# Four idle products of 128 columns in place of eight of 64, and one SwiGLU unit with two split chunks in place of ten

## The chip, the cores and the metric

The kernel runs on one core of a Trainium2 chip. Its engines work side by side, each through its own list of instructions in order, and wait for each other by semaphores: TensorE (matrix products; the profile calls its products PE and its weight loads PEld), VectorE (DVE), ScalarE (ACT), GpSimd (POOL) and SyncE (SP), which issues the transfers here. The metric is the device time of one execution in microseconds; of several runs the median is given.

## The reference

Two blocks read the same normalised input and are added to it: linear attention with a softmax feature map (A) and a SwiGLU block (B). S = 2048 tokens, D = 640, H = 32 heads of 20, F = 1536, all in bfloat16.

```
xn = layernorm(x)
q, k, v   = heads of xn @ wqkv
phi(u)    = [softmax(u @ w_phi), softmax(-(u @ w_phi))]      per head, 40 features
kv, z     = sum over tokens of phi(k) (x) v, and of phi(k)
o         = (phi(q) @ kv) / (phi(q) @ z + 1e-6)
out = x + (o @ wo) + (silu(xn @ w1) * (xn @ w3)) @ w2
```

## The kernel before

The tokens are 16 tiles of 128; a SwiGLU unit works on 512 tokens (a quarter) and 128 of the 1536 hidden columns, so there are 48 units. The input columns are 5 chunks of 128, over which each product accumulates in PSUM. The order of the work on every engine is written out by hand (`tc.manual_schedule`, line 156): what stands first in the text runs first on its engine.

The stages follow each other in this order.

- **Start and V.** The first tiles are loaded and transposed on TensorE (`by_pe`, line 294), their row statistics taken, and V is computed; the first three tiles use the raw input and are corrected later. While TensorE has nothing to do, it multiplies a tile of zeros into a bank that nobody reads: `warm(n, cols)`, line 219, issues n products with `cols` columns, 128 if not told otherwise. 40 of 64 columns stand ahead of the first tile (line 226) and 8 of 64 between the transposes of the first and second tile (line 766).
- **K stage** (line 908). For each of 16 tiles: the feature product, six exponentials on ScalarE, sum and reciprocal on VectorE, the scaling on GpSimd, and two tiles later the products that sum phi(k) and v. In between TensorE works off SwiGLU units.
- **Q stage** (line 936). The same feature product with the weights of q, for t = 0 to 15; the last two tiles of the K sum come at t = 0 and 1. For t = 0 to 6 two SwiGLU units follow each tile (lines 944 to 946). The first unit at t = 0 goes through `fill_halves(gate, up)`, line 710: it computes a unit like any other, but the last `gate` of the 5 chunks of the gate product, and the last `up` of those of the up product, are each done as two products of 256 columns in place of one of 512 (line 719). With 5 and 5 all chunks are split. All other units have products of 512 columns (line 459). After the products, ScalarE takes the tanh of the gate (line 470) and VectorE multiplies it together (lines 487 and 490).
- **Output.** Twelve tiles are computed in transposed pieces (`out_piece`, line 646), four tiles straight (`out_unit`, line 590). The very last tile is added and stored in three parts.
- **The branch** (line 999). A safeguard computes norms of the fused weights and, if they are too large, runs a second, general form of the attention. The flag is known long before the end, but the branch comes last: with these inputs every engine jumps over the general form to the last addition and store (`finish`, line 1025).

Each product is two instructions on TensorE, a weight load and the product itself. The split chunks use the same weights twice, and the weights are loaded for each half.

Of the kernel before, what the change touches and what calls it, by code (L numbers as in the profile page):

```python
# [8 lines left out]
P = 128  # L9
# [3 lines left out]
def kernel(  # L13
# [53 lines left out]
    def bank(name, dt=f32):  # L67
        n = 512 if dt == f32 else 1024
        return psum.tile([P, n], dt, name=name, tag="bank")
# [75 lines left out]
    def ld(dst, src):  # L145
        nc.sync.dma_start(out=dst, in_=src)
# [9 lines left out]
    with tc.manual_schedule():  # L156
# [62 lines left out]
        def warm(n, cols=P):  # L219
            for _ in range(n):  # L220
                nc.tensor.matmul(idle[:, 0:cols], nought[:], nought[:, 0:cols])
# [19 lines left out]
        def ln_stats(*ts):  # L241
            made = []
            for t in ts:
                xt = xin[:, (t // 4) % 3, t % 4, :]
                st = work.tile([P, 2, 6], f32, name="st")
                for i in range(2):
                    nc.vector.bn_stats(out=st[:, i, :], in_=xt[:, i * HD : (i + 1) * HD])  # L247
                made.append(st)
            for t, st in zip(ts, made):
                nc.vector.bn_aggr(out=mv[:, t, :], in_=st[:])  # L250
# [43 lines left out]
        def by_pe(dst, t, ps):  # L294
            xt = xin[:, (t // 4) % 3, t % 4, :]
            for c in range(KD):
                nc.tensor.transpose(
                    ps[:, c * P : (c + 1) * P], xt[:, c * P : (c + 1) * P], ident[:]
                )
            for c0, c1 in ((0, 2), (2, KD)):  # L300
                nc.scalar.copy(
                    out=dst[:, c0:c1, t * P : (t + 1) * P],
                    in_=ps[:, c0 * P : c1 * P].rearrange("p (c s) -> p c s", s=P),
                )
# [43 lines left out]
        def tile_of(t):  # L348
            return slice(t * P, (t + 1) * P)
# [61 lines left out]
        def phi_unit(t, w, name, exps=exps, cols=None):  # L411

            ps = by_token(cols or tile_of(t), w, name, CH)
            dst = phi[:, t % 4]
            exps(ps, dst)
            rows = dst.rearrange("p c g f -> p (c g) f")[:, :, 0:60].rearrange(
                "p a (i d) -> p a i d", d=Dh
            )
            sk = work.tile([P, 2 * NCH, 3], f32, name="sk")
            nc.vector.reduce_sum(out=sk[:], in_=rows, axis=AX.X)  # L420
            rk = work.tile([P, 2 * NCH, 3], f32, name="rk")
            nc.vector.reciprocal(out=rk[:], in_=sk[:])  # L422
            nc.gpsimd.tensor_mul(  # L423
                out=rows, in0=rows, in1=rk[:, :, :, None].to_broadcast([P, 2 * NCH, 3, Dh])
            )
# [28 lines left out]
        def glu_unit(sc, fi, banks=None):  # L454

            gp, up = banks or (bank("gp")[:], bank("up")[:])
            for ps, w in ((gp, w1), (up, w3)):
                for c in range(KD):
                    nc.tensor.matmul(  # L459
                        ps,  # L460
                        w[:, c, fi * P : (fi + 1) * P],
                        xnT[:, c, sc * 512 : (sc + 1) * 512],
                        start=(c == 0),
                        stop=(c == KD - 1),
                    )
            return glu_done(sc, fi, gp, up)

        def glu_done(sc, fi, gp, up):
            th = work.tile([P, 512], f32, name="th")
            nc.scalar.activation(out=th[:], in_=gp, func=AF.Tanh, scale=0.5)  # L470
            return lambda: glu_product(sc, fi, gp, up, th)
# [24 lines left out]
        def kv_unit(t, v1, acc, first, last):  # L496

            for c in range(NCH):
                b, i = divmod(c, 6)
                nc.tensor.matmul(  # L500
                    acc[:, b, VC * i : VC * i + 1 + Dh * HC[c]],
                    phi[:, t % 4, c].rearrange("p g f -> p (g f)"),
                    v1[:, c, 0 : 1 + Dh * HC[c]],
                    start=(first and i == 0),
                    stop=last,
                    skip_group_check=True,
                )
# [77 lines left out]
        def residual(rows):  # L585
            xr = work.tile([P, D], bf, name="xr")
            ld(xr[:], x2[rows, :])
            return xr
# [83 lines left out]
        def group_stored(g, i):  # L672
            rows = out2[(4 * g + 2 * i) * P : (4 * g + 2 * i + 2) * P, :]
            ld(
                rows.rearrange("(t p) d -> p t d", p=P),
                y[:, 2 * i : 2 * i + 2].rearrange("p t c s -> p t (c s)"),
            )
# [28 lines left out]
        def fill(n):  # L706
            for _ in range(n):
                glu_unit(*glu.pop(0))()

        def fill_halves(gate, up):  # L710

            sc, fi = glu.pop(0)
            gp, upp = bank("gp")[:], bank("up")[:]
            for ps, w, whole in ((gp, w1, KD - gate), (upp, w3, KD - up)):
                for c in range(KD):
                    n = 1 if c < whole else 2
                    for i in range(n):
                        a, b = i * 512 // n, (i + 1) * 512 // n
                        nc.tensor.matmul(
                            ps[:, a:b],  # L720
                            w[:, c, fi * P : (fi + 1) * P],
                            xnT[:, c, sc * 512 + a : sc * 512 + b],
                            start=(c == 0),
                            stop=(c == KD - 1),
                            skip_group_check=True,
                        )
            glu_done(sc, fi, gp, upp)()
# [35 lines left out]

        pst = [bank("pst", bf), bank("pst", bf)]
        by_pe(xrT, 0, pst[0])
        warm(8, P // 2)
        ln_stats(0)
        ln_root(0)
        by_pe(xrT, 1, pst[1])
# [166 lines left out]
        for t in range(NST + 4):  # L936
            if t < NST:
                phi_unit(t, wqphi, "pq")
            if t < 2:
                kv_unit(turns[t - 2], vaug[:, turns[t - 2]], acc, False, t == 1)  # L940
                if t == 1:
                    kv_done([acc[:, 0], acc[:, 1]])
                    ld(w2, B_w2.rearrange("(c p) d -> p c d", p=P))
            if t < 7:
                (fill_halves(5, 5) if t == 0 else fill(1))
                fill(1)
            for g, c in pieces.get(t, []):
                out_piece(g, c)
            outs = {16: (12,), 19: (13, 14, 15)}.get(t, ())
            for j in outs:  # L950
                last = tile_of(j) if j == NST - 1 else None
                res = out_unit(hT[:, j], tile_of(j % 4), xrs[j], last)
                if j == 13:
                    group_stored(2, 0)
                    group_stored(2, 1)
                if 13 <= j < 15:
                    xrs[j + 1] = residual(tile_of(j + 1))
                if last is None:
                    ld(out2[tile_of(j), :], res[:])
            if 2 <= t < NST + 2:  # L960
                r_unit(t - 2)
            if t < NST:
                phi_transposed(t)
            if 2 <= t < NST + 2:
                o_transposed(t - 2, (t - 2) // 4)
            if t in backs:
                group_back(*backs[t])
            if t in (12, 13):
                group_stored(0, t - 12)
            if t == 17:  # L970
                group_stored(1, 0)
            if 2 <= t < 6:
                x_back(t - 2)
            if 7 <= t < 11:
                x_back(t - 3)
            if 13 <= t < 17:
                x_back(t - 5)
            if t == 15:
                xrs[12] = residual(tile_of(12))
            if t == 17:  # L980
                xrs[13] = residual(tile_of(13))
            if t == 18:
                group_stored(1, 1)
                group_back(2, 0)
                group_back(2, 1)
            if t < 4:
                norm_unit(wqphi, 1, t)
            if t == 4:
                ld(listed[:], norms[:])
                ld(flat, listed[:].rearrange("p g -> (p g)").partition_broadcast(1))  # L990
            if t == 10:
                flag_unit()
            if t == 12:
                ok = nc.values_load(flag[0:1, 0:1], min_val=0, max_val=1)
# [59 lines left out]
```

## Time and profile before

| | us |
|---|---|
| median of 3 runs | 270.57 |
| lowest, highest | 268.92, 271.35 |
| the profiled execution | 268.92 |
| its span, first to last instruction | 267.2 |
| TensorE products, busy | 260.3 (97% of the span) |
| weight loads, busy | 153.9 (58%) |
| VectorE, ScalarE, GpSimd, busy | 193.1, 113.6, 90.6 |

The duration of a product includes a tail in which the next one is already running, so the time that a product takes in a row of products is the difference between two starts. A few records of products are missing from a trace: it has 1895 weight loads and 1869 products. The granted clock of TensorE is 1.000 in the mean of the span.

### The profile page before, as it was taken

To read this page: it belongs to the slowest core of one execution; us is meant where nothing else is said; L and a number is where in the kernel's file an instruction comes from. 1 tells how busy PE (TensorE), PEld (TensorE's weight loads), DVE (VectorE), ACT (ScalarE), POOL (GpSimd) and SP (SyncE) were. 2 spreads that over 40 slices of the span, in tenths; PEclk is the share of its full clock that TensorE was granted. 3 is DMA by queue.
4 is the path that set the end of the run, shared out by engine and by line. 5 is a ranking of instruction groups with operands and counts; after the bars stand their busy time and mean duration, and the time that the engine had idled before them with its cause. 6 is when DMAs were issued, how large, how long until landed. Compare 5 with 4: busy or idle time off the path is not lost.

```text
span 267.2 us, 5059 instructions
## 1 busy us (share of the span) xinstructions
PE 260.3 (97%) x1869; PEld 153.9 (58%) x1895; DVE 193.1 (72%) x356; ACT 113.6 (43%) x349; POOL 90.6 (34%) x83
## 2 busy tenths in 40 slices
PE   8999999999999999999999999999999999999993
PEld 7766465655556555555665555555555555544663
DVE  5899964397876877799879999998899685305121
ACT  5864354746668744466765554324222420000000
POOL 5022720064643544433553333346336433000000
PEclk9999999999999999999999999999999999999999
DMA  6958757984000002400009859456776999354861
GB/s 189 320 155 170 133 120 167 346 133 98 1 2 0 1 3 20 157 0 0 2 4 290 166 110 116 88 128 76 151 162 69 190 217 169 99 101 95 194 201 32
DMA packets 82828, 31.25 MB, mean 117 GB/s; under 512 B 71279, under 2 KB 81391, under 8 KB 82800
## 3 DMA queue, kind: packets, MB, share of 16 engines
q1 hardware_dynamic: 82800, 30.89, 52.1%
q8 instruction: 16, 0.26, 0.4%
q14 instruction: 12, 0.10, 0.1%
HBM read 11.17 MB, written 2.63 MB: 52 GB/s over the span
## 4 chain that ended last, share of the span: by engine, by line
PE 96%; DMA 1%; issue 1%; SPq 0%; DVE 0%
PE up L459 18%; PE gp L459 18%; PE acc L652 15%; PE pq L357 8%; PE pk L357 8%; PE acc L598 7%; PE pv L357 7%; PE acc L657 6%; PE pr L535 2%; PE pkv L500 2%; DMA reg_w<-in_A_wqkv_dram 1%; PE pf L443 1%; PE pv L308 1%; PE up L476 1%; PE gp L476 1%
## 5 line engine op out<-in xcount | busy, mean ns | idle before, releaser
L423 POOL TENSOR_TENSOR phi<-phi,rk 128x1320 bf16<-128x1320 bf16 x32 | 77.2, 2412 | 108.8 <-DVE rk L422 87.2
L459 PEld LDWEIGHTS <-w 128*128 128x128 bf16 x450 | 42.6, 97 | 46.9
L420 DVE TENSOR_REDUCE sk<-phi 128x66 f32<-128x1320 bf16 x32 | 48.8, 1525 | 19.6 <-ACT phi L386 18.3
L459 PE MATMUL up<-xnT,w 128*128 128x512 bf16 x225 | 55.9, 379 | 0.1
L459 PE MATMUL gp<-xnT,w 128*128 128x512 bf16 x206 | 54.3, 378 | 0.9
L357 PEld LDWEIGHTS <-xnT 128*128 128x128 bf16 x450 | 42.8, 98 | 19.2
L386 ACT ACTIVATE phi<-pq 128x360 bf16<-128x360 f32 (+2 forms) x96 | 24.8, 366 | 42.1 <-issue 31.8
L652 PE MATMUL acc<-reg_h,reg_v 128*128 128x512 bf16 x180 | 41.3, 379 | 0.0
L470 ACT ACTIVATE th<-gp 128x512 f32<-128x512 f32 x48 | 29.2, 611 | 26.8 <-PE gp L459 23.7
L490 DVE SCALAR_TENSOR_TENSOR reg_h<-gs,up 128x512 bf16<-128x512 bf16 x48 | 33.0, 688 | 5.4 <-PE pv L357 0.5
L487 DVE SCALAR_TENSOR_TENSOR gs<-th,gp 128x512 bf16<-128x512 f32 x48 | 31.4, 654 | 4.7 <-ACT th L470 4.7
L386 ACT ACTIVATE phi<-pk 128x360 bf16<-128x360 f32 (+2 forms) x96 | 24.9, 370 | 19.4 <-PE pk L357 19.4
L652 PEld LDWEIGHTS <-reg_v 128*128 128x128 bf16 x180 | 17.4, 98 | 19.1
L357 PE MATMUL pk<-wkphi,xnT 128*128 128x360 bf16 (+1 forms) x160 | 24.3, 299 | 0.0
L357 PE MATMUL pq<-wqphi,xnT 128*128 128x360 bf16 (+1 forms) x160 | 24.3, 299 | 0.0
L422 DVE RECIPROCAL rk<-sk 128x66 f32<-128x66 f32 x32 | 18.1, 566 | 3.2
L357 PE MATMUL pv<-reg_w,xnT 128*128 128x360 bf16 (+1 forms) x130 | 18.6, 299 | 0.0
L607 DVE TENSOR_TENSOR res<-acc,xr 128x320 bf16<-128x320 f32 (+3 forms) x9 | 3.8, 451 | 15.9 <-PE acc L598 10.5
L247 DVE BATCH_NORM_STATS2 st<-reg_h 128x6 f32<-128x320 bf16 x32 | 13.4, 479 | 2.1 <-DMA reg_h<-in_A_x_dram 2.1
L372 ACT CAST reg_v<-pv 128x360 bf16<-128x360 f32 (+2 forms) x39 | 10.7, 349 | 9.7 <-PE pv L357 9.7
L660 DVE TENSOR_TENSOR w<-acc,v_raw 128x512 bf16<-128x512 f32 x10 | 6.6, 671 | 11.2 <-issue 6.2
L556 DVE TENSOR_TENSOR o__77<-pr,den 128x360 bf16<-128x360 f32 (+1 forms) x32 | 14.2, 486 | 0.6
(90 smaller groups left out, 211.7 us busy)
## 6 DMA issues: line engine op xcount, KB each, us to landing
w<-in_B_w_dram SPq DMA_DIRECT2D x2, 1280.0 KB, 6.6
reg_v<-in_B_w_dram SPq DMA_DIRECT2D x1, 1920.0 KB, 8.9
out_dram<-w SPq DMA_DIRECT2D x6, 320.0 KB, 2.7
reg_h<-in_A_x_dram SPq DMA_DIRECT2D x5, 320.0 KB, 5.1
w<-in_B_w_dram SPq DMA_DIRECT2D x4, 320.0 KB, 6.8
reg_h<-in_A_x_dram SPq DMA_DIRECT2D x6, 160.0 KB, 2.5
reg_w<-in_A_wqkv_dram SPq DMA_DIRECT2D x5, 160.0 KB, 3.5
reg_w<-in_A_wo_dram SPq DMA_DIRECT2D x1, 800.0 KB, 7.5
```

The lines of the kernel that those rows point to most:

```text
L357: nc.tensor.matmul(ps[i][:, 0 : b - a], xnT[:, c, cols], w[:, c, a:b], start=(c == 0), stop=(c == KD - 1), skip_group_check=True,)
L386: nc.scalar.activation(out=dst[:, c0 : c0 + n, g, 0:k], in_=p.rearrange("p (c f) -> p c f", c=n), func=AF.Exp, scale=1.0 - 2.0 * g,)
L420: nc.vector.reduce_sum(out=sk[:], in_=rows, axis=AX.X)
L422: nc.vector.reciprocal(out=rk[:], in_=sk[:])
L423: nc.gpsimd.tensor_mul(out=rows, in0=rows, in1=rk[:, :, :, None].to_broadcast([P, 2 * NCH, 3, Dh]))
L459: nc.tensor.matmul(ps, w[:, c, fi * P : (fi + 1) * P], xnT[:, c, sc * 512 : (sc + 1) * 512], start=(c == 0), stop=(c == KD - 1),)
L470: nc.scalar.activation(out=th[:], in_=gp, func=AF.Tanh, scale=0.5)
L487: nc.vector.scalar_tensor_tensor(out=gs[:], in0=th[:], scalar=1.0, in1=gp, op0=ALU.add, op1=ALU.mult)
L490: nc.vector.scalar_tensor_tensor(out=hT[:, 4 * sc : 4 * sc + 4, fi, :], in0=gs[:].rearrange("p (t s) -> p t s", t=4), scalar=0.5, in1=up.r ...
L598: nc.tensor.matmul(ps[:, 0 : b - a], rows[j][0], rows[j][1][:, a:b], start=(j == 0), stop=(j == len(rows) - 1),)
L652: nc.tensor.matmul(acc4, w2[:, k, cols], hT[:, 4 * g : 4 * g + 4, k, :], start=(k == 0), stop=False,)
L657: nc.tensor.matmul(acc[:], wo[:, k, cols], oTs[g][:, k, :], start=False, stop=(k == KD - 1),)
```

## The change

Two calls change. Between the transposes of the first two tiles, four idle products of 128 columns are issued in place of eight of 64, the same 512 columns. In the first SwiGLU unit of the Q stage only the last chunk of the gate product and the last of the up product are split; the other four of each are whole. TensorE thus issues four idle products and eight SwiGLU products fewer, each with its weight load, and computes the same values. No other engine's instructions change.

```
         pst = [bank("pst", bf), bank("pst", bf)]
         by_pe(xrT, 0, pst[0])
-        warm(8, P // 2)
+        warm(4)
         ln_stats(0)
...
             if t < 7:
-                (fill_halves(5, 5) if t == 0 else fill(1))
+                (fill_halves(1, 1) if t == 0 else fill(1))
                 fill(1)
```

More of the change, by code (lines that the diff above doesn't have):

```diff
@@ L765 @@
         by_pe(xrT, 0, pst[0])
-        warm(8, P // 2)
+        warm(4)
         ln_stats(0)
@@ L944 @@
             if t < 7:
-                (fill_halves(5, 5) if t == 0 else fill(1))
+                (fill_halves(1, 1) if t == 0 else fill(1))
                 fill(1)
```

## The prediction

> **What bounds the kernel now.** I read the page's shares, its clock row and its chain first, then who waits for whom on TensorE, then the stretches between the first wait and the last product.
>
> ```profile
> PE 260.3 (97%) x1869; PEld 153.9 (58%) x1895; DVE 193.1 (72%) x356; ACT 113.6 (43%) x349; POOL 90.6 (34%) x83
> ...
> PEclk9999999999999999999999999999999999999999
> ...
> PE 96%; DMA 1%; issue 1%; SPq 0%; DVE 0%
> ```
>
> TensorE is busy for 97% of the span and carries 96% of the chain that ended last; no other engine is above 72%. So the time is the sum of TensorE's products, unless something makes TensorE stand. The view of waits, for TensorE alone, has two rows:
>
> ```profile
> PE idle L225 <- PEq L1038: 0.8, 1, 0.8
> PE v L308 <- DMA reg_w<-in_A_wqkv_dram: 0.3, 1, 0.3
> ```
>
> The first is the launch, the second the wait for a piece of the V weights near the start. The chain in order of time begins and ends like this (start, duration, what; the first two rows are neighbours, the last is the end):
>
> ```profile
> 2.18 3.20 DMA reg_w<-in_A_wqkv_dram
> 5.42 0.43 PE v L308 x2
> ...
> 262.86 0.26 DVE res L607
> ```
>
> Before 5.42 us the chain is the weight transfer, not the products. From then on it is TensorE to 262.83 us. The view of stretches (length, busy time and count of PE, PEld, DVE, ACT, POOL, granted clock, DMA share, GB/s) gives its two parts:
>
> ```profile
> 5.42:262.83 257.41, 256.02 (x1807) 149.95 (x1832) 190.55 (x347) 110.62 (x343) 87.39 (x65) 1.00 0.53 117
> 262.83:267.20 4.37, 0.00 (x0) 0.00 (x0) 0.26 (x1) 0.00 (x0) 0.00 (x0) 1.00 0.08 21
> ```
>
> In 257.41 us TensorE shows 1.39 us without a product, with 1832 weight loads and only 1807 products. Every product has its own load, so 25 products are missing from the records; with no wait recorded there, I read the 1.39 us as those and not as standing. The profiled execution took 268.92 us: 5.42 to the first product that waited, 257.41 of products, 4.37 for the last addition, the last store and the end, and 1.72 outside the span (268.92 - 267.20). It is the lowest of the three runs; the median is 270.57 and the highest 271.35, a spread of 2.43 us (0.9%) that this profile cannot explain, since it is of the lowest run.
>
> **Part one: the idle products of the start.** The view of instructions in order of time, TensorE alone (start, duration, engine, line, operation, what, count):
>
> ```profile
> 1.05 2.32 PE L221 MATMUL idle<-nought 128*128 128x64 bf16 x40
> 3.18 0.72 PE L297 MATMUL pst<-ident,reg_h 128*128 128x128 bf16 x5
> 3.69 0.63 PE L221 MATMUL idle<-nought 128*128 128x64 bf16 x8
> 4.14 0.66 PE L297 MATMUL pst<-ident,reg_h 128*128 128x128 bf16 x5
> 4.64 0.43 PE L308 MATMUL v<-reg_w 128*128 128x360 bf16 x2
> 5.42 0.43 PE L308 MATMUL v<-reg_w 128*128 128x360 bf16 x2 [0.35 <-DMA reg_w<-in_A_wqkv_dram]
> 5.69 0.43 PE L308 MATMUL pv<-reg_w 128*128 128x360 bf16 x2
> 5.96 0.44 PE L297 MATMUL pst<-ident,reg_h 128*128 128x128 bf16 x5
> 6.24 0.43 PE L308 MATMUL pv<-reg_w 128*128 128x360 bf16 x2
> ```
>
> Durations include a tail that overlaps the next product, so I take differences of starts. The eight products of 64 columns go from 3.69 to 4.14: 0.45 us. Four of 128 columns have no row before the change; five transposes of 128 columns do. On either side of the edit they take 0.51 us (3.18 to 3.69) and 0.50 (4.14 to 4.64), 0.10 each; a little later 0.28 (5.96 to 6.24), 0.056 each. TensorE thus works at about half its later rate until after 4.14 us, though the granted clock stands at 9 tenths or more in all 40 slices. Four products are between 4 x 0.056 = 0.22 and 4 x 0.102 = 0.41 us; I take 0.41, because the edit sits between two groups at the slow rate. The change is -0.04 us, within -0.23 and 0. It is worth nothing: the products at 4.64 run out of weights and TensorE then stands idle for 0.35 us until 5.42, a moment that the transfer sets. Anything saved is added to that idle time. If the transfer came earlier in another run, at most the 0.04 would show. The four weight loads that go with the four products lie under products as well.
>
> **Part two: the SwiGLU unit at the first Q tile.** Same view, TensorE, ScalarE and VectorE around the unit:
>
> ```profile
> 132.40 0.49 PE L500 MATMUL pkv<-reg_v,phi 128*128 128x61 bf16 x11
> ...
> 132.74 1.25 PE L719 MATMUL gp<-xnT,w 128*128 128x256 bf16 x10
> ...
> 133.83 1.25 PE L719 MATMUL up<-xnT,w 128*128 128x256 bf16 x10
> 134.03 0.60 ACT L470 ACTIVATE th<-gp 128x512 f32<-128x512 f32 x1
> 134.13 1.53 DVE L420 TENSOR_REDUCE sk<-phi 128x66 f32<-128x1320 bf16 x1 [0.33 <-ACT phi L386]
> ...
> 134.92 1.24 PE L459 MATMUL gp<-xnT,w 128*128 128x512 bf16 x4
> ...
> 136.00 1.24 PE L459 MATMUL up<-xnT,w 128*128 128x512 bf16 x5
> ...
> 136.24 0.63 DVE L487 SCALAR_TENSOR_TENSOR gs<-th,gp 128x512 bf16<-128x512 f32 x1
> ```
>
> Ten products of 256 columns take 133.83 - 132.74 = 1.09 us for the gate and 134.92 - 133.83 = 1.09 for the up half. The next unit, by five products of 512, takes 136.00 - 134.92 = 1.08. Splitting costs 0.01 us per five products (rows have two decimals, so 0 to 0.02). After the change four of the five chunks are whole and one is split: 0.8 of that goes, twice: -0.016 us, bounds -0.03 and 0. This is on the path, as TensorE has no gap here. Eight loads fewer lie under the products. What hangs on the unit does not move it: the tanh starts when the gate ends and is done at 134.63, while VectorE, busy with its sum from 134.13, takes up the result only at 136.24. No transfer is issued or moved, no wait is added, and no other engine's program changes.
>
> **The sum.** 0 - 0.016 = -0.02 us, against the profiled execution 268.90. Set on the median instead, 270.57 - 0.02 = 270.55; I say **270.5**.
>
> **What the sum leaves out: the instructions themselves.** Four and eight products go, each with its load: 24 TensorE instructions. The page lists the transfers that bring instructions, and the view of the final branch's line lists what the sequencers do there (count, shortest, median and longest ns, first and last start us); the last row is SyncE's longest wait at the end:
>
> ```profile
> q8 instruction: 16, 0.26, 0.4%
> ```
>
> ```profile
> L999 ACTq COMPARE_BRANCH  x1: 50/50/50, 217.8 to 217.8; - x1
> L999 ACTq EVENT_SEMAPHORE  x1: 17/17/17, 219.2 to 219.2; - x1
> L999 POOLq COMPARE_BRANCH  x1: 45/45/45, 221.5 to 221.5; - x1
> L999 POOLq EVENT_SEMAPHORE  x1: 17/17/17, 223.9 to 223.9; - x1
> L999 PEldq COMPARE_BRANCH  x1: 1295/1295/1295, 261.9 to 261.9; - x1
> ...
> L999 PEldq EVENT_SEMAPHORE  x1: 51/51/51, 263.2 to 263.2; - x1
> ```
>
> ```profile
> SPq L1049 <- DMA out_dram<-res: 2.1, 1, 2.1
> ```
>
> Sixteen packets carry 0.26 MB, 16 KB each; 0.4% of 16 engines' 267.2 us is 17.1 us, 1.07 us a packet. If they are TensorE's, its 2 x 1895 products and loads make some 69 bytes an instruction, and 24 instructions move every later packet boundary by a tenth of a packet. TensorE shows no wait at any boundary now. At the end its jump takes 1.3 us (261.9 to 263.2); on ScalarE the next instruction comes 1.4 us after the jump (217.8 to 219.2), on GpSimd 2.4 (221.5 to 223.9). Were TensorE's jump as long as GpSimd's, it would end 1.1 us later, and SyncE waits 2.1 us for the last store anyway: nothing. So I cost the moved boundaries at zero, with -1.3 (a jump or a fetch that disappears where it was uncovered) and +2.4 as ends. The Trainium skill, "Runtime: NRT & Kernel Launch", section "Instruction fetch mechanics", says that an engine's instructions come in blocks of 16 KiB, that crossing a block is mostly hidden, and that a taken branch whose target isn't loaded forces a fetch. The packet size and the times at the branch agree with it. By its figure of 256 instructions a block, 24 would be 0.09 of one, and its rule alone would let the end change by a fetch.
>
> **The rivals.**
>
> **A block comes late (slower).** The boundary lands where TensorE runs dry, in the products or at the jump beyond its cover. For it: 24 instructions shift all boundaries after 132 us, and the branch does cost its engines 1.3 to 2.4 us. Against it: 16 packets, no wait. Price 1.07 to 2.4 us, the lower end being likelier: 270.55 + 1.07 = 271.6, up to 273.0. It decides from the point where a stand passes the 2.1 us of cover at the end, or is in the products at all. Chance 0.13.
>
> **The slow start lasts longer (slower).** If fewer instructions in the first microseconds count as less work, the half rate stays. It lasts about 3.8 us now (0.84 to 4.64). Again as long would add half of that, 1.9 us, less up to 0.35 of idle time: 1.55 to 1.9, that is 272.1 to 272.5. Against it: TensorE is as busy as before, 0.41 of 0.45 us. Chance 0.08. The Trainium skill, "TensorE: Matmul & The Clock Gate", Part 1, section "What's actually happening", says that a free-running window of about 3.4 us of busy time, and not a number of instructions, opens the clock. By that the edit would do nothing, and the phase would vary a run by up to 1.7 us (an estimate, half of that window). The step after 3.8 us agrees; that the phase varies, no run here shows.
>
> **Fewer stands than before (faster).** The two higher runs of before may hold a stand that the profiled one lacks, and moved boundaries may avoid it: 268.9 to 269.3, up to -1.6. For it: the spread of 2.43 us. Against it: nothing in the profile places it. Chance 0.12.
>
> **How the numbers follow.** No change has 0.67, with runs between 268.9 and 271.4 as they were. A measurement of this kernel can tell about 1%, 2.7 us, from nothing. Slower by that needs 273.3: a stand at its upper end, or two of the slower cases together: 0.09 in all. Faster needs 267.9, below the profiled run even without its 0.35 us of idle time (268.55): 0.03. Within 1%: 0.88. The range goes from 268.6 (that idle time gone) to 272.4 (a slow start twice as long), leaving out the longest stands.
>
> **What would show it.** Right: line 221 with 44 products, line 719 with 4, the unit at 132.7 us 0.02 shorter, the first waited product again at 5.4, no TensorE wait after it, some 257.4 us to the last product. A late block would be a gap of about 1 us between two starts with no missing record, or a longer branch on line 999 followed by a later end; a longer slow start would be transposes at 0.10 us each after 5 us. The forecast is wrong if the products after 5.42 no longer follow each other without a gap, or the end after the last product is not 4.4 us.

## The result and the profile after

Over 18 runs each, the changed kernel takes 267.88 us in the median (267.35 to 269.31) and the kernel before 269.29 (268.36 to 271.35): a ratio of 0.9945, 95% interval 0.9927 to 0.9963. That is 1.4 us faster. The profiled execution of the changed kernel took 267.59 us, with 1.79 outside its span. The page of the changed kernel, span, first line of its busy times and engines of its chain:

```profile
span 265.8 us, 5035 instructions
...
PE 260.8 (98%) x1857; PEld 153.1 (58%) x1883; DVE 193.1 (73%) x356; ACT 113.7 (43%) x349; POOL 90.6 (34%) x83
...
PE 98%; issue 1%; DVE 0%
```

TensorE is as busy as before, so the 1.4 us did not come out of its products. The view of stretches, in the columns used above, cut at the end of the last product:

```profile
5.42:263.04 257.62, 256.22 (x1800) 148.93 (x1824) 190.50 (x347) 110.77 (x343) 87.40 (x65) 1.00 0.52 117
263.04:265.80 2.76, 0.00 (x0) 0.00 (x0) 0.26 (x1) 0.00 (x0) 0.00 (x0) 1.00 0.14 34
```

The row starts at 5.42 us to be comparable; the changed kernel has no wait for weights there in this execution. The last product ends 0.21 us later than before (263.04 against 262.83). Where it ends differs from execution to execution: over the profiles of all thirteen kernels here, 262.8 to 264.0 us. The end after it takes 2.76 us in place of 4.37: -1.61. The two make the -1.40 of the span. **The whole gain lies behind the last product**, where neither edit stands. The two edits themselves did what the sum said, in the view of instructions in time, first at the start, then around the unit:

```profile
3.69 0.63 PE L221 MATMUL idle<-nought 128*128 128x128 bf16 x4
...
4.12 0.74 PE L297 MATMUL pst<-ident,reg_h 128*128 128x128 bf16 x5
```

```profile
132.96 1.24 PE L719 MATMUL gp<-xnT,w 128*128 128x512 bf16 x6
134.04 1.25 PE L719 MATMUL up<-xnT,w 128*128 128x512 bf16 x6
135.12 1.24 PE L459 MATMUL gp<-xnT,w 128*128 128x512 bf16 x5
```

Four idle products take 0.43 us (eight took 0.45), and each half of the unit 1.08 (1.09 before).

What shrank at the end is the last store. In the lists of transfers (KB, us from issue to landing), before and then after:

```profile
out_dram<-res SPq DMA_DIRECT2D x1, 96.0 KB, 1.7
...
out_dram<-res SPq DMA_DIRECT2D x1, 64.0 KB, 3.2
```

```profile
out_dram<-res SPq DMA_DIRECT2D x1, 96.0 KB, 2.4
...
out_dram<-res SPq DMA_DIRECT2D x1, 64.0 KB, 1.5
```

The 64 KB of the last store took 3.2 us to land, and take 1.5 now. Before, the smaller store took nearly twice as long as the 96 KB one ahead of it. SyncE's wait for it, 2.1 us before, is down to 0.4, behind one of 0.2 for TensorE's jump:

```profile
SPq L1049 <- DMA out_dram<-res: 0.4, 1, 0.4
...
SPq L1049 <- PEq L999: 0.2, 1, 0.2
```

The transfers in a short window show why. Before, from 263.8 to 264.6 us and then from 264.6 to 266 (packets, and the queues with packets, MB and share of 16 engines):

```profile
DMA packets 136, 0.08 MB, mean 97 GB/s; under 512 B 15, under 2 KB 135, under 8 KB 135
...
q1 hardware_dynamic: 135, 0.06, 26.4%
q8 instruction: 1, 0.02, 10.3%
```

```profile
DMA packets 9, 0.00 MB, mean 3 GB/s; under 512 B 1, under 2 KB 9, under 8 KB 9
```

The store is 128 packets of data and 16 small ones, which makes nine for each of the 16 transfer engines. 135 of them went in the first window, together with one instruction packet on queue 8, and 10.3% of 16 engines' 0.8 us is 1.3 us for that one packet. Exactly nine packets, one engine's share, came afterwards, between 265.2 and 265.7 us. After the change, the same two windows:

```profile
DMA packets 144, 0.07 MB, mean 82 GB/s; under 512 B 16, under 2 KB 144, under 8 KB 144
...
q1 hardware_dynamic: 144, 0.07, 28.1%
```

```profile
q8 instruction: 1, 0.02, 5.8%
```

All 144 packets go through, and the instruction packet comes later, alone. It was put later by TensorE's jump over the general form (line 999; ns, first start us), which took 1295 ns before, and ends 1.2 us later now:

```profile
L999 PEldq COMPARE_BRANCH  x1: 2284/2284/2284, 262.1 to 262.1; - x1
...
L999 PEldq EVENT_SEMAPHORE  x1: 51/51/51, 264.4 to 264.4; - x1
```

So the reading is: TensorE, after its jump, orders one more packet of instructions of 16 KB. Before, that packet and the last store's share met on the same transfer engine, and the program's end waited for nine packets. The records of transfers don't name the engine; that it is one engine's share is read from the nine, and from their times. The packet lasts from 263.91 to 265.23 us, and the nine start at 265.22.

### The profile page after: what moved, and what is told of

Same layout as the page of the kernel before. It is cut to its first block, busy times and chain, and to the rows that moved or that the text cites. A ratio compares the mean times of both kernels' runs of the same rounds, so it can differ in the third digit from the quotient of the medians.

```text
span 265.8 us, 5035 instructions
## 1 busy us (share of the span) xinstructions
PE 260.8 (98%) x1857; PEld 153.1 (58%) x1883; DVE 193.1 (73%) x356; ACT 113.7 (43%) x349; POOL 90.6 (34%) x83
## 4 chain that ended last, share of the span: by engine, by line
PE 98%; issue 1%; DVE 0%
PE up L459 18%; PE gp L459 18%; PE acc L652 15%; PE pq L357 8%; PE pk L357 8%; PE acc L598 7%; PE pv L357 7%; PE acc L657 6%; PE pr L535 2%; PE pkv L500 2%; PE pf L443 1%; PE pv L308 1%; PE idle L221 1%; PE pst L297 1%; PE gp L476 1%; PE up L476 1%
```

## The experiments

**Theory F** (from the traces before and after): the count of TensorE instructions ahead of the jump decides when its next packets are ordered, and so whether the last one meets the last store. Rivals: **S**, the idle products at the start gained; **H**, the SwiGLU unit gained; and, for the later runs, that each instruction costs something. Ratios are to the kernel before on the same chip.

### Each edit alone

```
-        warm(8, P // 2)
+        warm(4)
```

> Only the four idle products of 128 for eight of 64: 8 TensorE instructions fewer than before. Theory F (an instruction packet of TensorE, 16 KB, starts about 0.7 us after its jump at the end and stands on one of the 16 DMA engines ahead of that engine's share of the last store; the number of instructions ahead of the jump decides when): the packet starts later than 263.9 us by 0.1 to 0.3, and partly misses the store; a time between the two kernels, 267.9 to 269.3, landing of the 64 KB store 1.5 to 3.2 us. Theory S (the start is what gained): all of the gain, -1.4 us, with the landing still 3.2 us. Theory H (the SwiGLU unit gained): 269.3, nothing.

Measured 269.20 us, ratio 1.0006 (0.9992 to 1.0020): nothing.

```profile
L999 PEldq COMPARE_BRANCH  x1: 1055/1055/1055, 262.4 to 262.4; - x1
```

```profile
out_dram<-res SPq DMA_DIRECT2D x1, 64.0 KB, 2.9
```

S falls. F expected part of the gain and there was none: the packet moved, but still into the store.

```
-                (fill_halves(5, 5) if t == 0 else fill(1))
+                (fill_halves(1, 1) if t == 0 else fill(1))
```

> Only the unit with two split chunks: 16 TensorE instructions fewer than before. Theory F: the block boundary is by my estimate about 12 instructions ahead of the jump before, so with 16 fewer it lies behind it; the jump takes about 2.3 us in place of 1.3, the packet starts after 265, the 64 KB store lands in 1.5 us: -1.4 us, about 267.9. Theory S: nothing, 269.3. Theory H: -1.4 us, with the landing still 3.2 us and the gain between 132 and 136 us.

Measured 267.67 us, ratio 0.9954 (0.9937 to 0.9972): within the intervals all of the gain.

```profile
L999 PEldq COMPARE_BRANCH  x1: 1795/1795/1795, 262.4 to 262.4; - x1
```

```profile
out_dram<-res SPq DMA_DIRECT2D x1, 64.0 KB, 1.5
```

The gain is in the landing, as F has it and H has not.

### The count put back elsewhere

```
-                (fill_halves(1, 1) if t == 0 else fill(1))
+                (fill_halves(*{0: (1, 1), 1: (5, 5), 2: (1, 1)}[t]) if t < 3 else fill(1))
```

> The changed kernel with the 24 instructions put back at other places: all ten chunks split in the first unit at t = 1 and two in the first at t = 2. Both edits stand as in the changed kernel. Theory F: the count ahead of the jump is that of before, so the time is that of before, about 269.3, landing about 3.2 us, jump 1.3 us. Theories S and H: the gain stays, 267.9.

Measured 268.93 us, ratio 0.9990 (0.9963 to 1.0017): with both edits standing, the gain is gone. H falls too. F was right on the time, but not on the rows: it expected a jump of 1.3 us and a landing of 3.2, and the profiled execution has 0.52 and 2.1. There the last product ends at 263.9 us, 1.1 later than in the profile of the kernel before, so the store starts later against the packet. Its data ends at 265.71 us against 265.68 before, since in both it waits for the packet, as shown further down. Of the 1.5 us by which its span is longer than that of the changed kernel, only 0.6 lie behind the last product; the ratio over 12 runs is what counts.

```profile
L999 PEldq COMPARE_BRANCH  x1: 515/515/515, 262.9 to 262.9; - x1
```

```profile
out_dram<-res SPq DMA_DIRECT2D x1, 64.0 KB, 2.1
```

### Only code that never runs is changed

These three kernels run every instruction of the kernel before, on all engines, and differ in what the jump passes over. First 240 TensorE instructions more there:

```
             kv_unit(0, v_one, acc, True, True)
+            unrun = bank("unrun")
+            for _ in range(120):
+                nc.tensor.matmul(unrun[:, 0:P], nought[:], nought[:])
```

> The kernel before, with 120 more idle products in the first loop of the general form, which these inputs jump over: 240 TensorE instructions that never run lie between the jump and its target; every instruction that runs is the same, on all engines. Theory F: the target moves one block further, which is not loaded at the jump; the jump takes 2.3 us or more, the packet after it starts after 265, landing 1.5 us: -1.4 us, about 267.9. Theories S and H, and any theory on what runs: 269.3.

Measured 268.71 us, ratio 0.9987 (0.9972 to 1.0002): the gain expected did not come.

```profile
L999 PEldq COMPARE_BRANCH  x1: 3507/3507/3507, 262.6 to 262.6; - x1
...
L999 PEldq EVENT_SEMAPHORE  x1: 51/51/51, 266.1 to 266.1; - x1
```

```profile
SPq L1052 <- PEq L999: 1.4, 1, 1.4
```

The store did land sooner (1.9 us), but one more packet is fetched (17 on queue 8). It comes from 263.6 to 264.6 us, starting 1.0 us after the jump began. So the jump took 3.5 us, and SyncE waited 1.4 us for TensorE instead of for the store. The cover at the end, named in the prediction, has its limit here. With 90 such instructions (45 products in the same place):

> As the run with 240 instructions that never run, but with 90: the target moves within the block that it is in (a packet holds some 240 instructions, 3817 over 16 packets). Theory F: jump 1.3 us, packet at 263.9, landing about 3 us, 269.1, no change. If it were the distance of the jump as such that counts, something between: TensorE's jump near 2.1 us and the end later.

Measured 268.89 us, ratio 0.9994 (0.9982 to 1.0006): no change, as F says. The jump takes 0.92 us although it passes over 90 instructions more, so its distance as such does not price it.

```profile
L999 PEldq COMPARE_BRANCH  x1: 915/915/915, 263.0 to 263.0; - x1
```

```profile
out_dram<-res SPq DMA_DIRECT2D x1, 64.0 KB, 2.4
```

And with 168 fewer (the general form's products cut):

```
-            v_unit(v_one, cols)
-            phi_unit(0, wkphi, "pk", exps_less_max, cols)
+            v_unit(v_one, cols, None, 2)
+            phi_unit(0, wkphi, "pk", exps_less_max, cols, 2)
...
-            phi_unit(0, wqphi, "pq", exps_less_max, rows)
+            phi_unit(0, wqphi, "pq", exps_less_max, rows, 2)
...
-            res = out_unit(h, slice(0, P), residual(rows))
+            res = out_unit(h, slice(0, P), residual(rows), None, KD)
```

> The kernel before, with the general form cut by 168 TensorE instructions: its products go over two of five chunks and its output leaves out the SwiGLU part; these inputs jump over all of it, and every instruction that runs is that of before, on all engines. Theory F: the target lies in the block that TensorE is in at the jump, some 12 instructions behind its start; the jump takes under 0.6 us and asks for no further block, so nothing meets the last store: landing 1.5 us, about 267.7 (-1.4). Any theory on the instructions that run: 269.1.

Measured 267.81 us, ratio 0.9956 (0.9941 to 0.9972): the gain of the change, with nothing that runs changed. One instruction packet is missing, the jump is short, and the store lands in 1.5:

```profile
L1000 PEldq COMPARE_BRANCH  x1: 242/242/242, 262.5 to 262.5; - x1
```

```profile
q8 instruction: 15, 0.25, 0.4%
...
out_dram<-res SPq DMA_DIRECT2D x1, 64.0 KB, 1.5
```

This also shows that queue 8 brings TensorE's instructions, since no other engine's program differs. No theory on the edits' own work has a place for this gain. That it is the packet and not the length of the jump follows with the changed kernel: there the jump is long (2.3 us), here it is short, and in both nothing meets the store and it lands in 1.5.

### Other counts

More instructions, 48 above the kernel before:

```
-                (fill_halves(5, 5) if t == 0 else fill(1))
+                (fill_halves(*{0: (5, 5), 1: (5, 5), 2: (5, 5), 3: (2, 2)}[t]) if t < 4 else fill(1))
```

> The kernel before with 48 TensorE instructions more: all chunks split in the first unit at t = 1 and 2 as well, two of each half at t = 3. Theory F: the next block is asked for some 2 to 3 us earlier and is there when TensorE jumps, so the jump takes under 0.6 us and the packet after it starts near 262 us, over before the last store (263.9 on): landing 1.5 us, about 268.0, -1.1 us although TensorE has 24 products more. A theory by which fewer instructions are better, or by which the two edits gain where they stand: 269.1 or 0.1 above.

Measured 268.28 us, ratio 0.9984 (0.9966 to 1.0001): a small gain at most, where F had expected 268.0 with a landing of 1.5. The jump is short as expected (the packet ahead arrived at 258.8), but it starts at 262.0 and the next packet runs from 263.1 to 264.2, not near 262: it still meets the beginning of the store.

```profile
L999 PEldq COMPARE_BRANCH  x1: 384/384/384, 262.0 to 262.0; - x1
```

```profile
out_dram<-res SPq DMA_DIRECT2D x1, 64.0 KB, 2.1
```

Twelve fewer (`fill_halves(2, 2)`), between the two edits' own counts:

> The kernel before with two split chunks per half in place of five: 12 instructions fewer, between the run with 8 (no gain) and the one with 16 (all of it). Theory F has the block boundary within these 8 instructions and says that the result is one of the two, not the middle: 269.0 with a jump of about 1 us and the packet near 264.5, or 267.8 with a jump of 1.8 us or more and the packet near 265. A theory by which each instruction counts: 268.4.

Measured 267.93 us, ratio 0.9973 (0.9947 to 0.9998). The profile, of a run of 267.63 us, has the long jump and the short landing:

```profile
L999 PEldq COMPARE_BRANCH  x1: 1739/1739/1739, 262.2 to 262.2; - x1
```

```profile
out_dram<-res SPq DMA_DIRECT2D x1, 64.0 KB, 1.5
```

F had said one of the two times and not the middle, and the single runs show both: seven of ten take 267.2 to 268.2 us, three 269.2 to 269.9. With this count the same kernel gains in some executions and not in others. That the three higher ones met the packet is not shown, since they have no trace.

48 fewer and 88 fewer, both edits of the changed kernel. For the second the tile of zeros is also made 256 columns wide, so that 40 idle products of 64 columns become 10 of 256:

```
-        warm(2 * WARM, P // 2)
+        warm(WARM - 4, P // 2)
+        warm(12)
```

> The changed kernel with 12 products fewer at the very start (24 of the 64-column idle products as 12 of 128): 48 instructions fewer than before, between the changed kernel (24, gain) and the one with 88 (no gain, TensorE itself late by a jump of 3.6 us). Theory F: the boundary is 36 instructions behind the jump; if the order for the next block runs that far ahead, 267.9 as the changed kernel; if not, jump 3.5 us, TensorE ends last at 266, 268.7. I take the second, 268.7, since the changed kernel's boundary is within 16 instructions of its jump. A theory by which fewer is better: under 267.9.

```
-        warm(2 * WARM, P // 2)
+        warm(WARM // 2, 2 * P)
...
-                (fill_halves(1, 1) if t == 0 else fill(1))
+                fill(1)
```

> The changed kernel with 64 instructions fewer still: the 40 idle products of 64 columns at the very start as 10 of 256 (the tile of zeros is 256 wide for it), and no split chunk left; 88 fewer than before. Theory F: the jump and its target then lie in one block and the next, which is loaded by then; the jump takes under 0.6 us, the packet starts near 262 us and is over before the last store: landing 1.5 us, 267.8, as the changed kernel or 0.1 below. A theory by which each instruction costs time: the gain grows with the count, 88 / 24 times 1.4 us, to 264.

Measured 268.83 us, ratio 0.9986 (0.9972 to 1.0001), and 268.76 us, 0.9998 (0.9986 to 1.0010): no gain in either. For 88 I had expected one. Both profiles show the same jump and the same last wait; of the kernel with 88 fewer:

```profile
L999 PEldq COMPARE_BRANCH  x1: 3632/3632/3632, 262.4 to 262.4; - x1
```

```profile
SPq L1049 <- PEq L999: 1.5, 1, 1.5
```

The packet ahead starts only after the jump has begun (by 1.0 and 1.2 us), and TensorE itself ends last. That each instruction costs time is ruled out: 24 fewer gain 1.4 us, 88 fewer nothing. For 88 fewer I had taken the jump and its target to lie in one block and the next, already loaded, and they don't. By my estimate, which no trace shows, the boundary lies some 12 instructions behind the jump in the changed kernel and 36 with 48 fewer; why the order comes in time in the first case and not in the second stays open.

Without the branch:

```
-    with tc.If(ok == 0) as general:
...
-    with general.Else():
-        nc.vector.memset(drift[:, 0:1], 0.0)
-        finish()
+    with tc.manual_schedule():
+        finish()
```

> The kernel before without the general form and without the branch: the last addition and store stand in line (the safeguard is left out). Theory F: TensorE has no jump and asks for no block near the last store, landing 1.5 us, 267.7 (-1.3) with the instructions before it those of before, 269.1 otherwise. It shows what the end is worth when nothing meets the store.

Measured 268.06 us, ratio 0.9963 (0.9950 to 0.9975); F had expected 267.7. Again 15 packets and a landing of 1.5. It is no better than the changed kernel, so the changed kernel has lost nothing to the branch that could still be had; no run beats it by more than the intervals.

```profile
q8 instruction: 15, 0.25, 0.4%
```

### All thirteen profiles together

The starts and ends of single packets, in the traces of the thirteen kernels, settle two things.

In eight of the profiled executions the last store met an instruction packet: before, the idle products alone, the count put back, 240 and 90 instructions more that never run, 48 more, 48 fewer and 88 fewer. In all eight the store's last data ended 0.45 us after the end of that packet, which lay anywhere from 264.2 to 265.6 us. In the five others (the changed kernel, the split chunks alone, 168 fewer that never run, 12 fewer, no branch) the data was through before any further packet came. From the last product to the end of the span these five take 2.7 us, and they are the five that gain; the eight take 3.3 to 4.4.

The packets also show what sets the length of the jump. In nine of the twelve kernels with a jump it ends 1.4 us after the packet ahead of it has arrived; in the three others it is under 0.6 us long, with that packet there. The next packet, where there is one, starts 0.7 to 1.1 us after the jump's end. Before, the packet ahead lasted from 260.81 to 261.75 us; in the changed kernel, with 24 instructions fewer ahead of it, from 261.99 to 262.98. This delay of 1.2 us is what put the last packet behind the store.

## Why the prediction was wrong

- **The bound and the two edits** were right: TensorE stands nowhere after 5.4 us, the idle products are worth nothing (0.43 us against 0.41 forecast), the unit gained 0.02. Two details were wrong. Line 719 shows 12 products after the change, since the whole chunks of the unit stand at that line as well, not 4. And the wait for weights at 5.4 us, which was to hide the start, is not there in the changed kernel; it comes and goes with the execution (0.9 us with the idle products alone, 0.5 with 168 fewer that never run, none in most others).
- **The step that failed** is "So I cost the moved boundaries at zero", and in it the cover: "SyncE waits 2.1 us for the last store anyway: nothing". I took that wait as something fixed that hides TensorE's jump. It was itself the cost: the packet that the jump orders kept the store open. The wait is 0.4 us in the changed kernel. I priced a packet only by TensorE standing for it, and not by what it does to a data transfer on the same engine. The rows were on the page: 64 KB in 3.2 us beside 96 KB in 1.7. The end of -1.3 that the text kept for the boundaries was nearly the size (-1.4), but by luck: it stood for a jump or a fetch that disappears, the jump grew by 1.0 us, and I gave that end no chance of its own.
- **The cover for TensorE's jump** was right in kind: with 2.3 us for the jump SyncE waits 0.2 us for it and then 0.4 more for the store, so it cost nothing; 3.5 to 3.6 us made TensorE the last (1.4 and 1.5 us of SyncE's wait).
- **The rivals.** A late block, slower: no run showed TensorE standing for one in the stream of products. A longer slow start: the half rate did last longer in the profiled execution, to about 5.4 us against 4.6, but no run ties that to the edit. A row of five transposes shows about 0.7 us at the half rate and 0.44 later: with the start as before, the run with the split chunks alone still has 0.67 at 6.25 us, and with the edited start the run with the idle products alone has 0.44 already at 3.87. So the length differs from execution to execution, of which the prediction had said that no run shows it. Fewer stands, faster: right in its sign and in its lever, the moved boundaries, wrong in its place; it spoke of TensorE, and of the higher runs only, while the meeting was in the profiled run too.
- **The base.** 270.5 was set on the median of three, 270.57; over 18 runs the kernel before has 269.29. Of the 2.6 us by which the forecast missed, 1.3 are this and 1.4 the gain. Set on the profiled execution, 268.92 - 0.02 = 268.90, it would have been off by 1.0.
- **Of the Trainium skill's rules**, "Runtime: NRT & Kernel Launch", section "Instruction fetch mechanics", has it that a taken branch to a target that isn't loaded forces a fetch. The runs agree and give it sizes: 0.24 us where the jump asked for no further packet, 0.4 to 1.3 where the packet ahead had arrived before the jump began, 1.7 to 2.3 where it was on its way, 3.5 to 3.6 where it started only 1.0 to 1.2 us after the jump had begun. That the packet ahead holds the target is read from these times. That crossing a block is mostly hidden holds for TensorE here; for a store that meets the block's packet it does not, by 1.7 us of landing.

## What to carry to other kernels

At the end of a kernel, where one small store is awaited, look at which instruction packets move in the same microsecond: a packet of 16 KB took 0.9 to 1.6 us at the end of these kernels, and the store was as late as the share that met it. A wait at the end that looks like cover for something else should first be asked why it is that long; a smaller transfer that lands later than a larger one of the same kind is the sign. Padding or cutting instructions far from the end, or code that never runs ahead of a jump's target, can gain or lose such a meeting; the window is narrow (12 to 24 instructions fewer gained here, 12 not in every run, and 8 and 48 did not), so it has to be measured again after any edit.

## What the runs showed of the hardware

That code which never runs changes the time was not in the prediction: 168 instructions cut from a skipped branch gave -0.44% (-0.59 to -0.28), 240 added turned the end from a wait for the store into a wait for TensorE's jump (3.5 us). The landing of one store of 64 KB was 1.5 us alone and 1.9 to 3.2 us when an instruction packet met it. Of the 1.7 us between the kernel before and the changed one, 1.35 lie ahead of the store's last data, by the times of the packets; the other 0.3 come behind it and are not explained. Nor is it explained what makes single runs of the kernel before reach 271 to 272 us: the last products of the profiled executions end within 1.1 us of each other.
